# Seven-product matmul stage: product sums kept in PSUM, turns and cosines passed through PSUM, two tiles split at once

## The chip, the cores and the metric

One NeuronCore of a Trainium2 chip runs the whole kernel. The metric is the device time of one execution in microseconds. "PE" is TensorE, "ACT" ScalarE, "DVE" VectorE, "POOL" GpSimd, "SP" SyncE, which here only issues DMAs. Each engine works off its own queue of instructions in program order; between engines, semaphores hold an instruction until its inputs are there and its output buffer is free.

## The reference

```python
rms = np.sqrt(np.mean(x * x, axis=-1, keepdims=True) + 1e-06)      # for q and k: x / rms * g
scores = (1 / np.sqrt(64)) * np.matmul(q_n, k_n.transpose(0, 1, 3, 2))
attn = softmax(scores);  attn_out = np.matmul(attn, v)             # 8 batches, 12 heads, 448 x 64
x = attn_out.transpose(0, 2, 1, 3).reshape(8 * 448, 768)
h = x @ w_in                                                        # 768 -> 2048
g = h * np.cos(h)
return g @ w_out                                                    # 2048 -> 768
```

All tensors are float32.

## The kernel before, in words

**Two stages.** The first stage does the attention of all eight batches (48 units of two heads) and, batch by batch, the first layer `h = x @ w_in`, whose 16 blocks of 128 x 448 per batch go to a DRAM tensor `h_d`. The first layer of the last batch stands at the head of the second stage (`ffn1_block`, 16 blocks of 18 matmuls). The second stage reads `h_d`, forms `g = h cos h`, and multiplies it by `w_out`.

**Float32 through splits.** A float32 operand is split into a high part in a rounded format, which ACT writes (a copy), and the low rest, which POOL writes (a subtraction of two SBUF tiles). A product of two operands is three matmuls: high-high, high-low, low-high (`ffn2`, lines 627 to 629).

**Seven products in place of eight.** Batches are taken in pairs (`pr`, four of them). The left-hand matrix (`w_out`, transposed) and the right-hand one (`g` of two batches) are each cut into 2 x 2 parts, and Strassen's scheme in Winograd's form makes the four output parts from seven products `pi`, each summing over 8 blocks `k`, for three output blocks `oc` of 128 rows. So there are 4 x 7 x 8 x 3 x 3 = 2016 matmuls. The four parts of `g` are the roles a, b, d, c; each has 8 blocks, held as four tiles of two blocks (128 x 896) with names `B{home}_{g}`. Sums and differences of the parts (`g_mix`, line 607) are written in place over tiles that are no longer needed. The combined weights of the seven products are prepared during the first stage (`weights2`: loads of 384 KB on SP, decoding on DVE and ACT, mixes and splits on POOL and ACT, stores to `wo_d`), and loaded from there (`v_place`, line 279, 768 KB each, into 16 slots that the first layer's weights have left). Products 0 and 1 keep their weights; those of the other five are loaded for each pair.

**One tile of g.** `gl_load` (line 577) brings two blocks of h into one of three `hb` buffers. `g_turns` (582, ACT) writes round(h / 2 pi) as integers to SBUF. `g_reduce` (589 and 594, DVE) subtracts the turns times 2 pi in two steps. `g_cos` (598 and 599, ACT) takes the absolute value and the sine of pi/2 minus it. `g_mul` (603, DVE) multiplies by h and so frees `hb`. Every one of these works on 128 x 896.

**Splits and outputs.** `g_split` (616 ACT, 614 POOL) splits one block of 448 at a time, in rings of five high and four low tiles. Each product's three sums have PSUM banks of their own out of a ring of eight. `e_copy` (646, ACT) copies three of the products to SBUF, `e_add` (651, 653, DVE) adds four others from PSUM to SBUF tiles, and `e_sum` (657, DVE) adds SBUF tiles to SBUF tiles, nine times per pair. `e_store` (661) stores the outputs.

**Order.** The order of the instructions on every engine is fixed beforehand by a planner (`Plan`): each part has an engine, a cost, a due time, the data that it reads and writes, and rings of buffers; a greedy simulation with these costs takes, whenever an engine is free, the part that is ready with the earliest due time. In the second stage a block of `k` is given 1.83 us on PE (`PART`), a product 14.64 us (`PROD`); `D[pi]` is when product `pi` is due.

Of the kernel before, what the change touches and what calls it, by code (L numbers as in the profile page):

```python
# [126 lines left out]
def tile_attention_moe(  # L127
# [452 lines left out]
    def g_turns(pr, role, g):  # L580
        n = blk[(pr, role, g, "n")] = gpool.tile([128, NG, S], I32, tag="n", name=f"n{pr}{role}{g}", bufs=RING2["n"])
        nc.scalar.activation(n, gts[(pr, role, g)], AF.Copy, scale=1.0 / (2.0 * math.pi))

    def g_reduce(pr, role, g, step):
        if step == 0:
            t = blk[(pr, role, g)] = gpool.tile(
                [128, NG, S], F32, tag=f"B{home(pr, role)}_{g}", name=f"B{pr}{role}{g}", bufs=1
            )
            nc.vector.scalar_tensor_tensor(  # L589
                t, blk[(pr, role, g, "n")], -C1, gts[(pr, role, g)], op0=ALU.mult, op1=ALU.add  # L590
            )
        else:
            t = blk[(pr, role, g)]
            nc.vector.scalar_tensor_tensor(t, blk.pop((pr, role, g, "n")), -C2, t, op0=ALU.mult, op1=ALU.add)  # L594

    def g_cos(pr, role, g):
        t = blk[(pr, role, g)]
        nc.scalar.activation(t, t, AF.Abs)
        nc.scalar.activation(t, t, AF.Sin, bias=halfpi, scale=-1.0)

    def g_mul(pr, role, g):
        t = blk[(pr, role, g)]
        nc.vector.tensor_tensor(t, t, gts.pop((pr, role, g)), ALU.mult)  # L603

    def g_mix(pr, to, a, c, g, eng):
        t = blk[(pr, to, g)]
        eng.tensor_tensor(t, blk[(pr, a, g)], blk[(pr, c, g)], ALU.subtract)  # L607

    def g_split(pr, pi, role, k, lo):
        t = gpool.tile([128, S], F32R, tag="glo" if lo else "ghi", name=f"g{lo}{pr}{pi}{k}", bufs=RING2["glo" if lo else "ghi"])  # L610
        ops[(pr, pi, k, lo)] = t
        src = blk[(pr, role, k // NG)][:, k % NG, :]
        if lo:
            nc.gpsimd.tensor_tensor(t, src, ops[(pr, pi, k, 0)].bitcast(F32), ALU.subtract)  # L614
        else:
            nc.scalar.copy(t, src)  # L616

    def ffn2(pr, pi, k, slot):
        hi, lo = ops.pop((pr, pi, k, 0)), ops.pop((pr, pi, k, 1))
        w = wts[("wo", slot)][:, k % 2]  # L620
        for oc in range(NO):
            if k == 0:
                ys[(pr, pi, oc)] = ps_y.tile([128, 512], F32, tag="y", name=f"y{pr}_{pi}_{oc}")
            y = ys[(pr, pi, oc)][:, :S]
# [2 lines left out]
            nc.tensor.matmul(y, whi, hi, start=(k == 0), stop=False)  # L627
            nc.tensor.matmul(y, whi, lo, start=False, stop=False)  # L628
            nc.tensor.matmul(y, wlo, hi, start=False, stop=(k == NH - 1))  # L629
# [15 lines left out]
    def e_copy(pr, pi, oc, name):
        nc.scalar.copy(e_tile(pr, name, oc), ys.pop((pr, pi, oc))[:, :S])

    def e_add(pr, pi, oc, to, a, op):
        y = ys.pop((pr, pi, oc))[:, :S]
        if op == ALU.add:  # L650
            nc.vector.tensor_tensor(e_tile(pr, to, oc), y, e_tile(pr, a, oc), op)  # L651
        else:
            nc.vector.tensor_tensor(e_tile(pr, to, oc), e_tile(pr, a, oc), y, op)

    def e_sum(pr, oc, to, a, eng):
# [1 line left out]
        eng.tensor_tensor(t, t, e_tile(pr, a, oc), ALU.add)  # L657
# [236 lines left out]
    count = iter(range(1000))  # L894
    split_n = iter(range(1000))

    def block(pr, role, g, d):
# [6 lines left out]
        add(ACT, 0.95, d - 20.0, g_turns, pr, role, g, r=[hb], w=[t])
        add(DVE, 1.15, d - 17.0, g_reduce, pr, role, g, 0, r=[hb, t], w=[B_])
        add(DVE, 1.15, d - 16.0, g_reduce, pr, role, g, 1, r=[t], w=[B_])
        add(ACT, 2.0, d - 14.0, g_cos, pr, role, g, w=[B_])
        add(DVE, 1.2, d - 11.0, g_mul, pr, role, g, r=[hb], w=[B_])

    def mix(pr, to, a, c, g, eng, d):  # L910
        e, cost = (nc.vector, 1.2) if eng == DVE else (nc.gpsimd, 2.4)
        add(eng, cost, d, g_mix, pr, to, a, c, g, e,
            r=[("B", home(pr, x), g) for x in (a, c) if x != to], w=[("B", home(pr, to), g)])

    def product(pr, pi, role):
        d0 = T0 + PROD * (NPR * pr + pi)
        for kk in range(NH // 2):
            if pi >= 2 or pr == 0:
                s = slot(pr, pi, kk)
                add(SP, ISS, d0 + 2 * PART * kk - 24.0, v_place, pr, pi, kk, s, w=[("w", s)], land=8.0)  # L920
        for k in range(NH):
# [1 line left out]
            n = next(split_n)
            B_, hi, lo = ("B", home(pr, role), k // NG), ("ghi", n), ("glo", n)
            add(ACT, 0.53, d - 7.0, g_split, pr, pi, role, k, 0, r=[B_], w=[hi])
            add(POOL, 1.25, d - 5.0, g_split, pr, pi, role, k, 1, r=[B_, hi], w=[lo])
# [4 lines left out]
    def Y(pr, pi, oc):
        return NFC + NO * (NPR * pr + pi) + oc

    def copies(pr, pi, name, d):
        for oc in range(NO):
            add(ACT, 0.53, d + oc, e_copy, pr, pi, oc, name, r=[("y", Y(pr, pi, oc))], w=[(name, oc)])

    def sums(pr, pi, to, a, op, d, where=None):
        for oc in range(NO):
            add(DVE, 0.65, d + oc, e_add, pr, pi, oc, to, a, op,  # L940
                r=[("y", Y(pr, pi, oc))] + ([(a, oc)] if a != to else []), w=[(to, oc)])
            if where:
                add(SP, ISS, d + oc + 1, e_store, pr, oc, to, *where, r=[(to, oc)], land=LAND)

    def more(pr, to, a, d, eng, where=None):
        e, cost = (nc.vector, 0.65) if eng == DVE else (nc.gpsimd, 1.25)
        for oc in range(NO):
            add(eng, cost, d + oc, e_sum, pr, oc, to, a, e, r=[(a, oc)], w=[(to, oc)])
# [3 lines left out]
    for pr in range(NPAIR):  # L952
        D = [T0 + PROD * (NPR * pr + pi) for pi in range(NPR + 1)]
        gs_ = range(NGR)
        for role, pi in (("a", 0), ("b", 1), ("d", 2), ("c", 5)):
            for g in gs_:
                block(pr, role, g, D[pi] + BLOCK * g - (9.0 if role != "a" else 0.0))
        copies(pr, 0, "e1", product(pr, 0, "a") + 2)
        for g in gs_:
            mix(pr, "a", "b", "a", g, DVE, D[1] + BLOCK * g - 10.0)  # L960
        copies(pr, 1, "e5", product(pr, 1, "a") + 2)
        for g in gs_:
            mix(pr, "b", "d", "b", g, POOL, D[2] + BLOCK * g - 12.0)
        copies(pr, 2, "e7", product(pr, 2, "b") + 2)
        for g in gs_:
            mix(pr, "a", "d", "a", g, DVE, D[4] + BLOCK * g - 14.0)
        sums(pr, 3, "e3", "e5", ALU.add, product(pr, 3, "d") + 2)
        d = product(pr, 4, "a") + 2
        sums(pr, 4, "u", "e1", ALU.add, d)
        more(pr, "e3", "u", d + 3, DVE, (0, 1))  # L970
        more(pr, "e7", "u", d + 5, DVE)
        more(pr, "e5", "e7", d + 7, DVE, (1, 1))
        for g in gs_:
            mix(pr, "a", "a", "c", g, DVE, D[6] + BLOCK * g - 14.0)
        sums(pr, 5, "e1", "e1", ALU.add, product(pr, 5, "c") + 2, (0, 0))
# [51 lines left out]
```

## Time and profile before

| | us |
|---|---|
| median of 3 runs | 1553.64 (1552.02 to 1555.42) |
| the profiled execution | 1550.64 |
| its span, first to last instruction | 1548.9 |
| first matmul of the last batch's first layer / of the seven products | 980 / 1038.6 |
| last matmul | 1545 |

Mean granted TensorE clock: 0.98 of full speed. The profile gives, for each group of instructions of one line, the count, the duration and who released the engine when it had been idle. `y<-g,wo` are the matmuls of the seven products, `ph<-xs,wi` those of the first layer, `B2c` is the tile of pair 2, role c, `n2c` its turns, `g<-B2c` its split, `es` and `e` are output tiles.

### The profile page before, as it was taken

How to read it: one execution, taken by the hardware profiler on the slowest of the kernel's cores; microseconds unless marked ns; L12 is line 12 of the kernel's file. 1: busy time of each engine (PE TensorE's matmuls, PEld its weight loads, DVE VectorE, ACT ScalarE, POOL GpSimd, SP SyncE). 2: the span in 40 equal slices, each digit the busy share in tenths (PEclk: the TensorE clock that was granted, in tenths of full speed). 3: DMA queues.
4: the chain of work that ended last, by engine and by line, in shares of the span. 5: the costliest groups of instructions: out<-in, count | busy, mean ns of one | idle time of the engine just before them, and what ended most of it. 6: DMA issues, size and time to landing. Idle time of an engine off the chain costs nothing. (4 is left out here: it accounts for less than half of the span.)

```text
span 1548.9 us, 23023 instructions
## 1 busy us (share of the span) xinstructions
PE 1441.8 (93%) x7404; PEld 1180.7 (76%) x7404; DVE 1224.9 (79%) x1935; ACT 993.9 (64%) x2022; POOL 1109.0 (72%) x862
## 2 busy tenths in 40 slices
PE   7898998999999999999999999998988998798799
PEld 3446886787788788788788888897777887687698
DVE  7878999888778777878785554469899899899944
ACT  5767776777677766777766664565655655575442
POOL 5778878888868776767774531219869978887975
PEclk9999999999999999999999999999989999999999
DMA  6577334666456555455453321691774566368153
GB/s 209 172 213 231 100 105 151 208 201 204 155 182 194 163 178 169 149 185 187 154 170 127 97 74 52 223 356 55 265 245 143 182 217 247 100 231 304 64 190 132
DMA packets 137961, 270.43 MB, mean 175 GB/s; under 512 B 20768, under 2 KB 89200, under 8 KB 137840
## 3 DMA queue, kind: packets, MB, share of 16 engines
q1 hardware_dynamic: 137840, 268.96, 53.0%
q8 instruction: 58, 0.95, 0.3%
q14 instruction: 63, 0.52, 0.1%
HBM read 206.18 MB, written 62.73 MB: 174 GB/s over the span
## 5 line engine op out<-in xcount | busy, mean ns | idle before, releaser
L628 PE MATMUL y<-g,wo 128*128 128x448 f32 x672 | 262.9, 391 | 47.5 <-POOL g L614 47.5
L554 PE MATMUL ph<-xs,wi 128*128 128x448 f32 x768 | 298.5, 389 | 2.6 <-ACT he L566 2.6
L555 PE MATMUL ph<-xs,wi 128*128 128x448 f32 x768 | 282.0, 367 | 0.0
L556 PE MATMUL ph<-xs,wi 128*128 128x448 f32 x768 | 281.5, 367 | 0.0
L448 ACT ACTIVATE P<-S,sm 128x448 f32<-128x448 f32 x336 | 213.9, 641 | 92.1 <-DVE S L435 82.8
L627 PE MATMUL y<-g,wo 128*128 128x448 f32 x672 | 254.5, 379 | 11.4 <-ACT g L616 11.4
L629 PE MATMUL y<-g,wo 128*128 128x448 f32 x672 | 254.3, 378 | 0.0
L435 DVE TENSOR_SCALAR_CACHE_REDUCE S<-S,nr 128x448 f32<-128x448 f32 x336 | 218.6, 684 | 17.7 <-PE S L428 16.4
L484 ACT CAST hi<-PT 128x448 fp32r<-128x448 f32 x336 | 164.7, 536 | 88.4 <-PE PT L473 48.8
L492 DVE TENSOR_TENSOR lo<-PT,hi 128x448 fp32r<-128x448 f32 x252 | 145.4, 616 | 78.9 <-ACT hi L484 75.5
L628 PEld LDWEIGHTS y<-g,wo 128*128 128x128 f32 x672 | 132.3, 197 | 79.7 <-POOL g L614 69.2
L473 PEld LDWEIGHTS PT<-ident,P 128*128 128x128 f32 x1344 | 157.9, 142 | 32.0 <-issue 20.3
L473 PE MATMUL PT<-ident,P 128*128 128x128 f32 x1344 | 182.0, 276 | 0.0
L554 PEld LDWEIGHTS ph<-xs,wi 128*128 128x128 f32 x768 | 144.9, 189 | 31.7 <-issue 12.3
L556 PEld LDWEIGHTS ph<-xs,wi 128*128 128x128 f32 x768 | 144.5, 188 | 12.6
L555 PEld LDWEIGHTS ph<-xs,wi 128*128 128x128 f32 x768 | 145.3, 189 | 9.6
L627 PEld LDWEIGHTS y<-g,wo 128*128 128x128 f32 x672 | 132.1, 197 | 25.4 <-ACT g L616 13.6
L306 POOL TENSOR_TENSOR r<-r,nhalf 128x14 f32<-128x14 f32 (+1 forms) x50 | 128.6, 2576 | 31.1 <-DVE r L302 17.1
L629 PEld LDWEIGHTS y<-g,wo 128*128 128x128 f32 x672 | 132.4, 197 | 10.4
L509 PE MATMUL O<-hi,vs 128*128 128x448 f32 x336 | 111.9, 383 | 8.4 <-DVE hi L494 5.2
L509 PE MATMUL O<-lo,vs 128*128 128x448 f32 x252 | 99.6, 404 | 17.0 <-DVE lo L492 16.5
L371 POOL TENSOR_TENSOR kl<-kd,khi 128x448 fp32r<-128x448 f32 x46 | 55.7, 1210 | 67.1 <-ACT khi L367 67.0
(224 smaller groups left out, 3157.9 us busy)
## 6 DMA issues: line engine op xcount, KB each, us to landing
wo<-wo_d SPq DMA_DIRECT2D x88, 768.0 KB
h_d<-he SPq DMA_DIRECT2D x128, 224.0 KB
hb<-h_d SPq DMA_DIRECT2D x64, 448.0 KB
wo_d<-wv SPq DMA_DIRECT2D x56, 384.0 KB
sd<-sd SPq DMA_DIRECT2D x46, 448.0 KB
vd<-v SPq DMA_DIRECT2D x84, 160.0 KB
qd<-qT SPq DMA_DIRECT2D x48, 256.0 KB
raw<-w_in SPq DMA_DIRECT2D x16, 768.0 KB
```

Source lines behind the costliest of these rows:

```text
L435: nc.vector.tensor_scalar(d["S", t][:, :S], d["S", t][:, :S], d["nr"][:, t : t + 1], None, op0=ALU.mult, op1=ALU.min, accum_out=d["sm"][:, ...
L448: nc.scalar.activation(tl(u, f"P{t}", [128, S], F32, "P"), d.pop(("S", t))[:, :S], AF.Exp, bias=sm[:, 1, t : t + 1], scale=-1.0, accum_out ...
L473: nc.tensor.transpose(pt[:, t * 128 : t * 128 + 128], src, ident)
L484: nc.scalar.copy(hi, pt[:, hh * S : hh * S + S])
L492: nc.vector.tensor_tensor(lo, src, hi.bitcast(F32), ALU.subtract)
L509: nc.tensor.matmul(O, st, d.pop((what, kb, hh)), start=(kc + n == 0), stop=(kc + n == 4))
L554: nc.tensor.matmul(ph[:, :S], whi, x2[:, 0, :], start=(cc == 0), stop=False)
L555: nc.tensor.matmul(ph[:, :S], whi, x2[:, 1, :], start=False, stop=False)
L556: nc.tensor.matmul(ph[:, :S], wlo, x2[:, 0, :], start=False, stop=(cc == NCC - 1))
L627: nc.tensor.matmul(y, whi, hi, start=(k == 0), stop=False)
L628: nc.tensor.matmul(y, whi, lo, start=False, stop=False)
L629: nc.tensor.matmul(y, wlo, hi, start=False, stop=(k == NH - 1))
```

## The change

The seven products are taken in another order (1, 7, 6, 2, 5, 4, 3 in place of 1, 5, 7, 3, 6, 2, 4). Product 0 starts a sum in one set of three PSUM banks; products 2, 4 and 6 go on adding to that same sum (`CHAIN` is 2: no start flag), and it is read in between. Products 1, 3 and 5 start afresh in the other set. The two sets change places with each pair. There are 6 named banks for sums (the first layer uses them too) in place of a ring of 8.

The two banks left over hold the turns and the cosines of one block of 448 at a time: ACT writes them to PSUM, and DVE reads them from there. Only the absolute value is still taken on 896. The SBUF tiles for turns go.

Splits take two blocks (128 x 896) at once, in rings of three. The additions of SBUF tiles to SBUF tiles for the outputs go; in the last pair the last output tile is copied in two halves by ACT and DVE. One of the four mixes is now an addition; the one on POOL is the last one (a - c), where it was d - b. The blocks b and d are due together, 18 us ahead of product 1, c 12 us ahead of product 3. The weights of the second stage are prepared from unit 18 to unit 46 of the plan in place of 12 to 45.

```diff
-    ORDER = (1, 5, 7, 3, 6, 2, 4)
+    ORDER = (1, 7, 6, 2, 5, 4, 3)
...
-            ffn1(b, fc, part, ps_y, "y")
+            ffn1(b, fc, part, ps_y, f"y{fc % NB}")
...
-    def g_turns(pr, role, g):
-        n = blk[(pr, role, g, "n")] = gpool.tile([128, NG, S], I32, tag="n", name=f"n{pr}{role}{g}", bufs=RING2["n"])
-        nc.scalar.activation(n, gts[(pr, role, g)], AF.Copy, scale=1.0 / (2.0 * math.pi))
+    def g_turns(pr, role, g, f):
+        n = gts[(pr, role, g, f)] = ps_g.tile([128, 512], I32, tag="n", name=f"n{pr}{role}{g}{f}")
+        nc.scalar.activation(n[:, :S], gts[(pr, role, g)][:, f, :], AF.Copy, scale=1.0 / (2.0 * math.pi))
...
+        t = blk[(pr, role, g)][:, f, :]
+        n = gts[(pr, role, g, f)][:, :S]
+        src = t if step else gts[(pr, role, g)][:, f, :]
+        nc.vector.scalar_tensor_tensor(t, n, -C2 if step else -C1, src, op0=ALU.mult, op1=ALU.add)
+
+    def g_abs(pr, role, g):
         t = blk[(pr, role, g)]
         nc.scalar.activation(t, t, AF.Abs)
-        nc.scalar.activation(t, t, AF.Sin, bias=halfpi, scale=-1.0)
+
+    def g_cos(pr, role, g, f):
+        c = gts[(pr, role, g, f)] = ps_g.tile([128, 512], F32, tag="c", name=f"c{pr}{role}{g}{f}")
+        nc.scalar.activation(c[:, :S], blk[(pr, role, g)][:, f, :], AF.Sin, bias=halfpi, scale=-1.0)
+
+    def g_mul(pr, role, g, f):
+        c, h = gts.pop((pr, role, g, f)), gts[(pr, role, g)][:, f, :]
+        nc.vector.tensor_tensor(blk[(pr, role, g)][:, f, :], c[:, :S], h, ALU.mult)
...
+    def g_split(pr, pi, role, g, lo):
+        name = "glo" if lo else "ghi"
+        t = ops[(pr, pi, g, lo)] = gpool.tile([128, NG, S], F32R, tag=name, name=f"{name}{pr}{pi}{g}", bufs=RING2[name])
+        src = blk[(pr, role, g)]
         if lo:
-            nc.gpsimd.tensor_tensor(t, src, ops[(pr, pi, k, 0)].bitcast(F32), ALU.subtract)
+            nc.gpsimd.tensor_tensor(t, src, ops[(pr, pi, g, 0)].bitcast(F32), ALU.subtract)
...
-            nc.tensor.matmul(y, whi, hi, start=(k == 0), stop=False)
-            nc.tensor.matmul(y, whi, lo, start=False, stop=False)
-            nc.tensor.matmul(y, wlo, hi, start=False, stop=(k == NH - 1))
+            nc.tensor.matmul(y, whi, hi, start=(k == 0 and chain < 2), stop=False, skip_group_check=chain == 2)
+            nc.tensor.matmul(y, whi, lo, start=False, stop=False, skip_group_check=chain == 2)
+            nc.tensor.matmul(y, wlo, hi, start=False, stop=(k == NH - 1), skip_group_check=chain == 2)
...
-    def e_sum(pr, oc, to, a, eng):
-        t = e_tile(pr, to, oc)
-        eng.tensor_tensor(t, t, e_tile(pr, a, oc), ALU.add)
...
-        span = (base(NU - NP // 2) - base(2 * NP)) / NH
-        d0 = base(2 * NP) + k * span
+        span = (base(NU - 2) - base(3 * NP)) / NH
+        d0 = base(3 * NP) + k * span
...
-    RING2 = {"he": 2, "hb": 3, "n": 2, "ghi": 5, "glo": 4, "y": 8}
+    RING2 = {"he": 2, "hb": 3, "ghi": 3, "glo": 3, "n": 1, "c": 1}
+    CHAIN = (0, 1, 2, 1, 2, 1, 2)
...
+        return 3 if role == "b" else ("acd".index(role) + pr) % 3
+
+    def bank(pr, pi, oc):
+        return NO * ((pr + CHAIN[pi] % 2) % 2) + oc
...
+        for f in range(NG):
+            t = ("n", NG * n + f)
+            add(ACT, 0.56, d - 20.0 + 1.5 * f, g_turns, pr, role, g, f, r=[hb], w=[t])
+            add(DVE, 0.63, d - 19.0 + 1.5 * f, g_reduce, pr, role, g, f, 0, r=[hb, t], w=[B_])
+            add(DVE, 0.63, d - 18.5 + 1.5 * f, g_reduce, pr, role, g, f, 1, r=[t], w=[B_])
+        add(ACT, 0.96, d - 15.0, g_abs, pr, role, g, w=[B_])
+        for f in range(NG):
+            c = ("c", NG * n + f)
+            add(ACT, 0.57, d - 13.0 + 1.5 * f, g_cos, pr, role, g, f, r=[B_], w=[c])
+            add(DVE, 0.63, d - 12.0 + 1.5 * f, g_mul, pr, role, g, f, r=[hb, c], w=[(*B_, f)])
...
+        for roles, pi, ahead in (("a", 0, 12.0), ("bd", 1, 18.0), ("c", 3, 12.0)):
+            for g in range(NGR):
+                for n, role in enumerate(roles):
+                    block(pr, role, g, D[pi] + BLOCK * g - ahead + 2 * n)
+        d = product(pr, 0, "a")
+        mix(pr, "b", "d", "b", ALU.subtract, D[1] - 12.0)
+        copies(pr, 0, "e1", d + 1)
+        mix(pr, "a", "b", "a", ALU.add, D[2] - 14.0)
+        d = product(pr, 1, "b")
+        copies(pr, 1, "e7", d + 1)
+        d = product(pr, 2, "a")
+        mix(pr, "b", "d", "a", ALU.subtract, D[3] - 10.0)
+        sums(pr, 2, "u3", "e7", d + 1)
+        mix(pr, "a", "c", "a", ALU.subtract, D[3] - 2.0, POOL)
+        d = product(pr, 3, "c")
+        sums(pr, 3, "e1", "e1", d + 1, (0, 0))
+        d = product(pr, 4, "b")
+        sums(pr, 4, "c22", "e7", d + 1, (1, 1))
+        d = product(pr, 5, "a")
+        sums(pr, 5, "u3", "u3", d + 1, (1, 0))
+        d = product(pr, 6, "d")
+        copies(pr, 6, "c12", d + 1, (0, 1))
```

More of the change, by code (lines that the diff above doesn't have):

```diff
@@ L587, in g_reduce @@
+    def g_reduce(pr, role, g, f, step):
+        if (step, f) == (0, 0):
+            blk[(pr, role, g)] = gpool.tile(
                 [128, NG, S], F32, tag=f"B{home(pr, role)}_{g}", name=f"B{pr}{role}{g}", bufs=1
             )
[L589 to L594, printed above, removed]
@@ L618, in ffn2 @@
     def ffn2(pr, pi, k, slot):
-        hi, lo = ops.pop((pr, pi, k, 0)), ops.pop((pr, pi, k, 1))
+        hi, lo = (ops[(pr, pi, k // NG, x)][:, k % NG, :] for x in range(2))
         w = wts[("wo", slot)][:, k % 2]
+        chain = CHAIN[pi]
         for oc in range(NO):
-            if k == 0:
-                ys[(pr, pi, oc)] = ps_y.tile([128, 512], F32, tag="y", name=f"y{pr}_{pi}_{oc}")
-            y = ys[(pr, pi, oc)][:, :S]
+            bk = bank(pr, pi, oc)
+            if k == 0 and chain < 2:
+                ys[bk] = ps_y.tile([128, 512], F32, tag=f"y{bk}", name=f"y{pr}_{pi}_{oc}")
+            y = ys[bk][:, :S]
             whi = w[:, 0, oc * 128 : oc * 128 + 128]
             wlo = w[:, 1, oc * 128 : oc * 128 + 128]
-            nc.tensor.matmul(y, whi, hi, start=(k == 0), stop=False)
-            nc.tensor.matmul(y, whi, lo, start=False, stop=False)
-            nc.tensor.matmul(y, wlo, hi, start=False, stop=(k == NH - 1))
+            nc.tensor.matmul(y, whi, hi, start=(k == 0 and chain < 2), stop=False, skip_group_check=chain == 2)
+            nc.tensor.matmul(y, whi, lo, start=False, stop=False, skip_group_check=chain == 2)
+            nc.tensor.matmul(y, wlo, hi, start=False, stop=(k == NH - 1), skip_group_check=chain == 2)
     es = {}
@@ L641, in e_tile, with e_copy, e_add @@
                     es["t"] = xpool.tile([128, 2 * NCC, S], F32, tag="xs", name="es")
-                es[(pr, name, oc)] = es["t"][:, NO * ("e7", "e3", "u").index(name) + oc, :]
+                es[(pr, name, oc)] = es["t"][:, NO * ("u3", "c12", "c22").index(name) + oc, :]
         return es[(pr, name, oc)]
[L645 to L651, printed above, removed]
-        else:
-            nc.vector.tensor_tensor(e_tile(pr, to, oc), e_tile(pr, a, oc), y, op)
-    def e_sum(pr, oc, to, a, eng):
-        t = e_tile(pr, to, oc)
-        eng.tensor_tensor(t, t, e_tile(pr, a, oc), ALU.add)
+    def e_copy(pr, pi, oc, name, hf=None):
+        t, y = e_tile(pr, name, oc), ys[bank(pr, pi, oc)][:, :S]
+        if hf is not None:
+            t, y = (x[:, hf * S // 2 : hf * S // 2 + S // 2] for x in (t, y))
+        if hf == 1:
+            nc.vector.tensor_copy(t, y)
+        else:
+            nc.scalar.copy(t, y)
+    def e_add(pr, pi, oc, to, a):
+        nc.vector.tensor_tensor(e_tile(pr, to, oc), ys[bank(pr, pi, oc)][:, :S], e_tile(pr, a, oc), ALU.add)
     def e_store(pr, oc, name, i, j):
@@ L886, in tile_attention_moe @@
         d = BLOCK * fc
-        add(PE, BLOCK, d, ffn1_block, B - 1, fc, w=[("y", fc), ("w", fc)])
-        add(ACT, 0.53, d + 4.0, h_out, B - 1, fc, r=[("y", fc)], w=[("he", fc)])
+        y = ("y", fc % NB)
+        add(PE, BLOCK, d, ffn1_block, B - 1, fc, w=[y, ("w", fc)])
+        add(ACT, 0.53, d + 4.0, h_out, B - 1, fc, r=[y], w=[("he", fc)])
         add(SP, ISS, d + 5.0, h_store, B - 1, fc, r=[("he", fc)], w=[("hd", B - 1, fc)], land=LAND)
@@ L892, in slot @@
         return 4 * pi + kk if pi < 2 else 8 + (20 * pr + 4 * (pi - 2) + kk) % 8
-    count = iter(range(1000))
-    split_n = iter(range(1000))
+    count, split_n = iter(range(1000)), iter(range(1000))
     def block(pr, role, g, d):
@@ L899, in block, with block_keys, mix @@
         n = next(count)
-        hb, t = ("hb", n), ("n", n)
-        B_ = ("B", home(pr, role), g)
+        hb, B_ = ("hb", n), ("B", home(pr, role), g)
         r = [("hd", 2 * pr + j, NH * i + NG * g + f) for f in range(NG)]
         add(SP, ISS, d - 30.0, gl_load, pr, role, g, r=r, w=[hb], land=LAND)
[L904 to L913, printed above, removed]
+        for f in range(NG):
[8 more added lines that the diff above has]
+            add(DVE, 0.63, d - 12.0 + 1.5 * f, g_mul, pr, role, g, f, r=[hb, c], w=[(*B_, f)])
+    def block_keys(pr, role, g):
+        B_ = ("B", home(pr, role), g)
+        return [B_] + [(*B_, f) for f in range(NG)]
+    def mix(pr, to, a, c, op, d, eng=DVE):
+        e, cost = (nc.vector, 1.2) if eng == DVE else (nc.gpsimd, 2.3)
+        for g in range(NGR):
+            add(eng, cost, d + BLOCK * g, g_mix, pr, to, a, c, g, op, e,
+                r=sum((block_keys(pr, x, g) for x in (a, c) if x != to), []), w=block_keys(pr, to, g))
     def product(pr, pi, role):
@@ L919, in product @@
                 s = slot(pr, pi, kk)
-                add(SP, ISS, d0 + 2 * PART * kk - 24.0, v_place, pr, pi, kk, s, w=[("w", s)], land=8.0)
+                add(SP, ISS, d0 + BLOCK * kk - 24.0, v_place, pr, pi, kk, s, w=[("w", s)], land=8.0)
         for k in range(NH):
             d = d0 + PART * k
[L923 to L926, printed above, removed]
+            g = k // NG
@@ L927, in product @@
+            if k % NG == 0:
+                n = next(split_n)
+                Bs, hi, lo = block_keys(pr, role, g), ("ghi", n), ("glo", n)
+                add(ACT, 0.96, d - 8.0, g_split, pr, pi, role, g, 0, r=Bs, w=[hi])
+                add(POOL, 2.3, d - 6.0, g_split, pr, pi, role, g, 1, r=Bs + [hi], w=[lo])
             s = slot(pr, pi, k // 2)
-            add(PE, PART, d, ffn2, pr, pi, k, s, r=[hi, lo, ("w", s)], w=[("y", Y(pr, pi, oc)) for oc in range(NO)])
+            add(PE, PART, d, ffn2, pr, pi, k, s, r=[hi, lo, ("w", s)], w=[("y", bank(pr, pi, oc)) for oc in range(NO)])
@@ L929, in product, with copies @@
         return d0 + PROD
-    def Y(pr, pi, oc):
-        return NFC + NO * (NPR * pr + pi) + oc
-    def copies(pr, pi, name, d):
+    def copies(pr, pi, name, d, where=None):
         for oc in range(NO):
-            add(ACT, 0.53, d + oc, e_copy, pr, pi, oc, name, r=[("y", Y(pr, pi, oc))], w=[(name, oc)])
-    def sums(pr, pi, to, a, op, d, where=None):
-        for oc in range(NO):
[L940 to L948, printed above, removed]
+            y = ("y", bank(pr, pi, oc))
+            if where and pr == NPAIR - 1 and oc == NO - 1:
+                add(ACT, 0.3, d + oc, e_copy, pr, pi, oc, name, 0, r=[y], w=[(name, oc)])
+                add(DVE, 0.35, d + oc, e_copy, pr, pi, oc, name, 1, r=[y], w=[(name, oc, 1)])
+            else:
+                add(ACT, 0.53, d + oc, e_copy, pr, pi, oc, name, r=[y], w=[(name, oc)])
@@ L949, in more, with sums @@
+            if where:
+                add(SP, ISS, d + oc + 1, e_store, pr, oc, name, *where, r=[(name, oc), (name, oc, 1)], land=LAND)
+    def sums(pr, pi, to, a, d, where=None):
+        for oc in range(NO):
+            add(DVE, 0.63, d + oc, e_add, pr, pi, oc, to, a,
+                r=[("y", bank(pr, pi, oc))] + ([(a, oc)] if a != to else []), w=[(to, oc)])
             if where:
@@ L953, in tile_attention_moe @@
         D = [T0 + PROD * (NPR * pr + pi) for pi in range(NPR + 1)]
[L954 to L975, printed above, removed]
-        sums(pr, 6, "e7", "e7", ALU.subtract, product(pr, 6, "a") + 2, (1, 0))
+        for roles, pi, ahead in (("a", 0, 12.0), ("bd", 1, 18.0), ("c", 3, 12.0)):
+            for g in range(NGR):
+                for n, role in enumerate(roles):
[18 more added lines that the diff above has]
+        copies(pr, 6, "c12", d + 1, (0, 1))
     with tc.manual_schedule():
```

26 lines of the change are left out of this document (8 added, 18 removed).

## The prediction

> **What bounds the kernel now.** First the page's share of the span by engine and its 40 slices; then busy time by stage, the waits of the second stage, single lines, and the timeline at one wait.
>
> ```profile
> PE 1441.8 (93%) x7404; PEld 1180.7 (76%) x7404; DVE 1224.9 (79%) x1935; ACT 993.9 (64%) x2022; POOL 1109.0 (72%) x862
> PE   7898998999999999999999999998988998798799
> DVE  7878999888778777878785554469899899899944
> ```
>
> PE is at 93%, but a matmul's busy time overlaps the next one's, so I count matmuls per stretch (the x after PE). Columns: stretch, its length, busy time of PE, PEld, DVE, ACT, POOL, granted clock, DMA share, GB/s.
>
> ```profile
> 240.00:260.00 20.00, 15.39 (x82) 12.02 (x83) 19.23 (x36) 13.44 (x31) 19.25 (x17) 1.00 0.49 150
> 260.00:280.00 20.00, 17.10 (x91) 13.88 (x90) 17.46 (x34) 12.62 (x29) 16.46 (x15) 1.00 0.49 159
> 355.00:829.00 474.00, 463.49 (x2610) 382.89 (x2610) 364.65 (x799) 336.58 (x782) 352.43 (x326) 0.99 0.55 173
> 440.00:460.00 20.00, 20.00 (x116) 16.72 (x115) 15.46 (x38) 14.19 (x32) 11.16 (x11) 1.00 0.57 185
> 980.00:1038.60 58.60, 58.60 (x285) 53.21 (x284) 33.45 (x30) 38.22 (x52) 7.84 (x5) 1.00 0.93 324
> 1038.60:1545.20 506.60, 447.71 (x2018) 390.73 (x2016) 436.47 (x295) 277.70 (x420) 413.75 (x236) 0.95 0.54 185
> 1520.00:1540.00 20.00, 20.00 (x101) 18.53 (x100) 8.57 (x9) 5.41 (x10) 13.18 (x11) 1.00 0.27 97
> ```
>
> The change's home is 1038.6 to 1545.2: 2016 matmuls of the 28 products. Undisturbed matmuls follow each other so:
>
> ```profile
> 1538.13 0.36 PE L629 MATMUL y<-g,wo 128*128 128x448 f32 x1
> ...
> 1544.21 0.36 PE L629 MATMUL y<-g,wo 128*128 128x448 f32 x1
> ```
>
> Thirty matmuls in 6.08 us: 0.2027 apart. 2016 × 0.2027 = 408.6; the stage takes 506.6, so 98.0 us are lost in it. Who holds PE there (waiter, what it waited for, us, times, longest):
>
> ```profile
> PEld y L628 <- POOL g L614: 69.2, 74, 4.1
> POOL g L614 <- ACT g L616: 53.1, 26, 7.4
> PEld y L627 <- ACT g L616: 13.6, 6, 3.7
> ```
>
> 82.8 us of waiting, and behind a wait the clock is slow as well (the stage's mean grant is 0.95):
>
> ```profile
> 1206.97 0.37 PE L627 MATMUL y<-g,wo 128*128 128x448 f32 x1
> 1210.10 0.47 PE L628 MATMUL y<-g,wo 128*128 128x448 f32 x1 [2.76 <-POOL g L614]
> ...
> 1210.97 0.57 PE L628 MATMUL y<-g,wo 128*128 128x448 f32 x1
> ...
> 1213.58 0.57 PE L629 MATMUL y<-g,wo 128*128 128x448 f32 x1
> ```
>
> Seven matmuls in 2.61 us are 0.373 apart. So the splits come late, because POOL and ACT are late, because of DVE. Columns: min/median/max in ns.
>
> ```profile
> L589 DVE SCALAR_TENSOR_TENSOR B0b<-n0b,hb x4: 1086/1092/1092, 1011.4 to 1027.7; 128x896 f32<-128x896 int32 x4
> L589 DVE SCALAR_TENSOR_TENSOR B0c<-n0c,hb x4: 1720/2032/3011, 1066.5 to 1089.5; 128x896 f32<-128x896 int32 x4
> L607 DVE TENSOR_TENSOR B1a<-B1b,B1a x4: 2035/2042/2555, 1168.5 to 1187.2; 128x896 f32<-128x896 f32 x4
> L607 POOL TENSOR_TENSOR B1b<-B1d,B1b x4: 2142/2956/2961, 1171.5 to 1205.2; 128x896 f32<-128x896 f32 x4
> L614 POOL TENSOR_TENSOR g<-B1a,g x32: 1149/1996/2024, 1164.1 to 1290.3; 128x448 fp32r<-128x448 f32 x32
> L657 DVE TENSOR_TENSOR es<-es x24: 611/1570/1580, 1137.3 to 1521.6; 128x448 f32<-128x448 f32 x24
> L651 DVE TENSOR_TENSOR es<-y,e x24: 605/610/625, 1117.8 to 1516.0; 128x448 f32<-128x448 f32 x24
> L492 DVE TENSOR_TENSOR lo<-PT,hi x252: 601/615/626, 124.5 to 963.8; 128x448 fp32r<-128x448 f32 x126
> ```
>
> The same DVE operation takes 1.09 us while POOL is nearly idle (before 1038) and 2.03 beside POOL's splits; POOL's take 1.15 or 2.00. Each slows the other when DVE reads two SBUF tiles. With one operand in PSUM (L651, L492) DVE never passes 0.626, whatever POOL does. The bound of the stage is this mutual slowing: DVE is busy 86% of it, POOL 82%.
>
> **The change, part by part**, per pair of batches (7 products, 504 matmuls, 102.2 us of PE; now 506.6/4 = 126.65).
>
> *Turns and cosines through PSUM.* 16 blocks had 48 DVE operations on 896 elements; now 96 on 448 with the turn or cosine read from PSUM. No row has scalar_tensor_tensor on integers from PSUM. Nearest are L651's 0.610 and, against it, L657's 1.570 (two SBUF tiles): I take 0.613, as one operand is in PSUM. 96 × 0.613 = 58.8 us. Undisturbed, two halves cost 1.22 against 1.09, so alone this adds 0.13 × 48 = 6.2 us; it pays only through the disturbance. [...]
>
> *Mixes.* Twelve on DVE (2.04 each beside POOL: 24.5) and four on POOL, as before; another one is POOL's.
>
> *Sums in PSUM.* L657 goes, nine a pair; the 12 additions from PSUM stay: 7.4. The banks of one product are written again two products later. Three copies or additions have the product between (14.6 us) as cover; without it PE would wait for three of 0.6.
>
> DVE per pair: 58.8 + 24.5 + 7.4 = 90.7, against (33.5 + 436.5)/4 = 117.5.
>
> *Splits of two tiles.* POOL: 28 of 896. Not shown; L607's 2.14 at the least disturbed and twice 1.149 are near: 2.3. With four mixes 74, plus 10 for those running beside 24.5 us of DVE mixes (24.5 × (1 − 1.15/2.0)): 84, against 105.4. ACT:
>
> ```profile
> L314 ACT ACTIVATE PT<-sd x4: 547/548/548, 3.4 to 12.1; 128x448 f32<-128x448 f32 x4
> L598 ACT ACTIVATE B0a<-B0a x4: 952/954/956, 987.4 to 1007.5; 128x896 f32<-128x896 f32 x4
> L599 ACT ACTIVATE B0a<-B0a,halfpi x4: 1045/1047/1047, 989.7 to 1008.5; 128x896 f32<-128x896 f32 x4
> L646 ACT COPY e<-y x24: 521/530/547, 1059.2 to 1476.9; 128x448 f32<-128x448 f32 x24
> ```
>
> 28 × 0.954 + 32 × 0.548 (turns, written to PSUM) + 16 × 0.954 + 32 × 0.60 (half a sine, in L599's ratio) + 9 × 0.53 = 83. PE's 102.2 becomes the longest.
>
> *New waits.* One bank for turns, one for cosines: a turn waits until both reductions of the half before it have read the bank; behind it in ACT's queue stand the splits that PE needs. Hand-over shows as 0.09 us (ACT to DVE):
>
> ```profile
> 1417.98 0.95 ACT L582 ACTIVATE n3d<-hb 128x896 int32<-128x896 f32 x1 [1.02 <-DMA hb<-h_d]
> ...
> 1419.02 1.09 DVE L589 SCALAR_TENSOR_TENSOR B3d<-n3d,hb 128x896 f32<-128x896 int32 x1 [1.19 <-ACT n3d L582]
> ```
>
> A half holds its bank 0.55 + 1.23 + 0.18 = 1.96 us; 32 make 63 of 102, hidden unless DVE has something longer ahead. The splits' rings (three of two tiles) give 11 us of cover; if that is gone, PE waits and then runs at 0.373.
>
> Blocks b and d are now due together, 18 us ahead of product 1, and c 12 ahead of product 3: eight loads of hb stand in SP's queue in a row, among the weight loads. Pair 0 has the 58.6 us of first-layer matmuls as cover (DVE 33.5 busy there), the others the three products since their homes came free; if that is gone, product 1 waits for its first mix. The mix left to POOL (a − c, 2.3 each) queues ahead of splits; the same 11 us cover it.
>
> *Weights of the second stage* are prepared later and more tightly (span 66.5 for 78.4 in the plan, six attention units later): 32 loads and 56 stores on SP, 88 POOL, 128 DVE and 88 ACT operations move with it. At the old start PE made 82 and 91 matmuls for 116 in 20 us: 5.9 + 4.3 = 10.2 us lost. Ends: all of it regained (−10), or lost twice (+10); I take −3, since later stretches have DVE freer. Their last store moves by some 19 us from 829, far ahead of the second stage.
>
> *Order of products, bank names:* nothing; the loads of weights only change slots. *Tail:* the last tile is copied in halves, 0.3 us less.
>
> *Sum.* Residual loss: in 355 to 829, with DVE 77% busy, PE made 2610 of the 2749 that 116 per 20 us allow: 5.1% lost. With DVE at 89% of PE's time I take between as much and half as much again, 6.3%: 408.6/0.937 = 436. Span: 1548.9 − (506.6 − 436) − 3 − 0.3 = 1475.0; with the 1.7 us around it (1550.64 − 1548.9) 1476.7. The profiled execution is 3.0 under the median of the runs, 1553.64; I put the forecast between the two scales, **1478**. Its own range is 1450 (no loss: 1548.9 − 98 − 3 + 1.7) to 1500.
>
> **Rivals.** *A: the hb ring binds.* Three buffers; a load's passage:
>
> ```profile
> 1410.48 7.47 DMA hb<-h_d
> 1418.02 10.37 DMA hb<-h_d
> ```
>
> ```profile
> SPq L577 <- DVE B2c L603: 27.9, 4, 16.1
> ```
>
> 7 to 10 us until it is used, then 7.7 us of its own work (two turns 1.1, four reductions 2.45, 0.95, 2 × 1.2, nine hand-overs 0.8), and what stands ahead in the queues. It decides once a passage is over 19.2 us (3 × 102.2/16). With 10.4 + 7.7 + two mixes of 2.04 it is 22.2, 118 us a pair, 473 for the stage: 1514. For it: loads queue behind 768 KB weight loads. SP already waits up to 16.1 us for a product to free a buffer. Against: those passages were stretched by a slow DVE.
>
> *B: no relief, slower.* The reductions on integers keep taking the shared path. 64 × 1.57 + 32 × 0.613 + 24.5 + 7.4 = 152 us of DVE a pair; scaled by 126.65/117.5 the pace is 164, +149 in all: about 1700. It turns from faster to slower once the 96 halves average over 0.89 us ((117.5 − 31.9)/96). Against: 252 + 24 rows from PSUM, none over 0.626. [...]
>
> *C: the change does not do what it says*: splits stay the bound, POOL at 896 elements being disturbed as a whole, 4 us each: 28 × 4 + 10 = 122 us a pair, about today's 126.65: 1550. Against: DVE reads two SBUF tiles in only 24.5 of 102 us.
>
> **How the numbers follow.** Forecast 0.67, A 0.2, B 0.06, C 0.07. Holding eight in ten means the forecast's range and most of A: 1450 to 1516. The runs of before spread over 3.4 us, 0.2%, which is what can be told from no change. Faster: 0.67 + 0.2 + 0.03 of C = 0.90; same 0.03; slower 0.07.
>
> **What would show it.** Right: reductions and products near 0.61 each, splits on POOL near 2.3, at least 95 matmuls per 20 us in most stretches, DVE below 90%, clock above 0.97 in the second stage, no L657. Wrong: halves at 1 us or more (B); POOL's splits at 3 or more (C); loads of hb waiting long for the products that free them, and turns waiting for them (A); or ACT's turns standing for DVE with PE's waits shifted from POOL to ACT.

## The result, and the profile after

The changed kernel takes 1458.64 us (median of 4 runs, 1457.63 to 1460.19) where the kernel before takes 1553.37 beside it: a ratio of 0.939, with a 95% interval of 0.9374 to 0.9406. The forecast was 1478, in a range of 1450 to 1516; the profiled execution is 1460.19, its span 1458.2. First the page: busy time by engine, and the slices of PE, DVE and POOL.

```profile
PE 1408.1 (97%) x7404; PEld 1167.4 (80%) x7404; DVE 1069.7 (73%) x2092; ACT 1001.4 (69%) x2038; POOL 973.9 (67%) x750
PE   6898999999999999999999999999999999999998
DVE  7878999678788687878687756536876876976821
POOL 5779779777787867796787573101296596685674
```

The holes at the end of PE's line are gone, although PE does the same work. The same stretches as before, with the same columns (stretch, length, busy time of PE, PEld, DVE, ACT, POOL with their counts, granted clock, DMA share, GB/s):

```profile
1030.80:1454.20 423.40, 415.66 (x2018) 379.43 (x2016) 288.93 (x425) 283.00 (x421) 278.29 (x125) 1.00 0.66 222
1132.00:1236.00 104.00, 102.38 (x506) 94.54 (x505) 80.17 (x121) 77.81 (x118) 71.43 (x32) 1.00 0.73 247
1160.00:1180.00 20.00, 18.38 (x91) 16.71 (x90) 17.30 (x24) 15.82 (x25) 16.68 (x7) 1.00 0.39 120
240.00:260.00 20.00, 17.92 (x95) 13.76 (x95) 15.51 (x36) 16.09 (x37) 19.83 (x18) 1.00 0.45 134
260.00:280.00 20.00, 19.66 (x112) 16.09 (x112) 14.00 (x31) 12.64 (x30) 14.43 (x13) 1.00 0.51 157
355.00:829.00 474.00, 465.20 (x2619) 384.14 (x2618) 371.15 (x815) 342.63 (x794) 359.66 (x332) 1.00 0.57 181
```

The first row is the product stage: 423.4 us for the 2016 matmuls that took 506.6, so 83.2 of the 90.7 us that the span lost are here. The stage starts 7.8 us earlier (1030.8 for 1038.6); the 82 and 91 matmuls of the two stretches from 240 to 280 have become 95 and 112. DVE's busy time in the stage fell from 436 to 289 us, POOL's from 414 to 278, and the granted clock rose from 0.95 to 1.00. The second row is about one pair of batches (506 matmuls). Next, single lines by count, min/median/max in ns:

```profile
L592 DVE SCALAR_TENSOR_TENSOR B1a<-n1a,hb x8: 610/620/625, 1080.1 to 1098.7; 128x448 f32<-128x448 int32 x8
L592 DVE SCALAR_TENSOR_TENSOR B1a<-n1a,B1a x8: 624/624/626, 1080.8 to 1099.3; 128x448 f32<-128x448 int32 x8
L604 DVE TENSOR_TENSOR B1a<-c1a,hb x8: 611/618/625, 1087.3 to 1105.8; 128x448 f32<-128x448 f32 x8
L607 DVE TENSOR_TENSOR B1a<-B1b,B1a x4: 1081/1089/1478, 1136.1 to 1163.3; 128x896 f32<-128x896 f32 x4
L607 DVE TENSOR_TENSOR B1b<-B1d,B1a x4: 1079/1914/2979, 1155.2 to 1168.9; 128x896 f32<-128x896 f32 x4
L614 POOL TENSOR_TENSOR glo<-B1a,ghi x12: 2120/2130/2993, 1132.8 to 1220.4; 128x896 fp32r<-128x896 f32 x12
```

Every operation that reads a turn or a cosine from PSUM takes 0.61 to 0.63, whatever POOL does. The mixes, which still read two SBUF tiles, stand at 1.09 when POOL is between splits and reach 2.98 beside one; a split reaches 2.99. Most of them now miss each other. What PE still waits for in the stage (waiter, released by, us in total, times, longest):

```profile
PEld y L630 <- POOL glo L614: 8.7, 4, 2.9
PEld y L629 <- ACT ghi L616: 0.9, 1, 0.9
```

Before, POOL's splits held it for 69.2 us. One of the four waits in the timeline (start, duration, engine, operation):

```profile
1163.29 3.01 POOL L614 TENSOR_TENSOR glo<-B1b,ghi 128x896 fp32r<-128x896 f32 x1 [6.46 <-ACT ghi L616]
...
1163.27 1.08 DVE L607 TENSOR_TENSOR B1a<-B1b,B1a 128x896 f32<-128x896 f32 x1
1164.27 2.98 DVE L607 TENSOR_TENSOR B1b<-B1d,B1a 128x896 f32<-128x896 f32 x1
...
1166.35 0.47 PE L630 MATMUL y<-glo,wo 128*128 128x448 f32 x1 [1.62 <-POOL glo L614]
```

The first mix began 0.02 us before the split and took its 1.08 us undisturbed; the split took 0.88 over its 2.13. The second mix began during the split and ended 0.95 us after it (1167.25 against 1166.30), about a whole mix later. In these rows they take turns, and the matmul that needs the split is 1.62 us late. In the third window row above (1160 to 1180) that shows as 91 matmuls where the stretch after it has 100.

### The profile page after: what moved, and what is told of

It reads as the page before. It is cut to its first block, busy times and chain, and to the rows that moved or that the text cites. A ratio compares the mean times of both kernels' runs of the same rounds, so it can differ in the third digit from the quotient of the medians.

```text
span 1458.2 us, 22829 instructions
## 1 busy us (share of the span) xinstructions
PE 1408.1 (97%) x7404; PEld 1167.4 (80%) x7404; DVE 1069.7 (73%) x2092; ACT 1001.4 (69%) x2038; POOL 973.9 (67%) x750
## 4 chain that ended last, share of the span: by engine, by line
PE 70%; DVE 11%; ACT 4%; issue 3%; POOL 3%; DMA 1%; SPq 0%; ACTq 0%; DVEq 0%; POOLq 0%
PE ph L554 9%; PE ph L555 8%; PE ph L556 8%; PE O L509 8%; PE y L630 8%; PE y L631 8%; PE y L629 7%; PE PT L473 7%; PE S L428 6%; DVE S L435 2%; ACT hi L484 1%; DVE lo L492 1%; DVE hi L494 1%; DVE xf L526 1%; POOL glo L614 1%
## 5 line engine op out<-in xcount | busy, mean ns | idle before, releaser
L448 ACT ACTIVATE P<-S,sm 128x448 f32<-128x448 f32 x336 | 213.8, 640 | 92.9 <-DVE S L435 83.2
L630 PE MATMUL y<-glo,wo 128*128 128x448 f32 x672 | 247.4, 368 | 7.3 <-POOL glo L614 7.3
L629 PE MATMUL y<-ghi,wo 128*128 128x448 f32 x672 | 247.1, 368 | 0.5 <-ACT ghi L616 0.5
L631 PE MATMUL y<-ghi,wo 128*128 128x448 f32 x672 | 247.0, 368 | 0.0
L630 PEld LDWEIGHTS y<-glo,wo 128*128 128x128 f32 x672 | 126.6, 188 | 20.2 <-POOL glo L614 8.7
L629 PEld LDWEIGHTS y<-ghi,wo 128*128 128x128 f32 x672 | 126.6, 188 | 12.3 <-ACT ghi L616 0.9
L631 PEld LDWEIGHTS y<-ghi,wo 128*128 128x128 f32 x672 | 126.6, 188 | 11.4
L428 PE MATMUL S<-khi,qhi 64*128 64x448 f32 (+1 forms) x350 | 99.9, 491 | 1.5 <-ACT khi L343 1.2
```

What stands on the lines that cost most here:

```text
L428: nc.tensor.matmul(d["S", t][:, :S], d[a][p0:p1, j * 128 : j * 128 + 128], d[c][p0:p1, :], start=(n == 0), stop=(n == len(ops) - 1),)
L448: nc.scalar.activation(tl(u, f"P{t}", [128, S], F32, "P"), d.pop(("S", t))[:, :S], AF.Exp, bias=sm[:, 1, t : t + 1], scale=-1.0, accum_out ...
L629: nc.tensor.matmul(y, whi, hi, start=(k == 0 and chain < 2), stop=False, skip_group_check=chain == 2)
L630: nc.tensor.matmul(y, whi, lo, start=False, stop=False, skip_group_check=chain == 2)
```

## The experiments

Unless said otherwise, ratios are to the kernel before on the same chip, with their 95% interval.

**Is it the route through PSUM?** Both turns and cosines back in SBUF, all else as changed:

```diff
-        n = ... ps_g.tile([128, 512], I32, tag="n", ...)
+        n = ... gpool.tile([128, S], I32, tag="n", ..., bufs=1)
-        c = ... ps_g.tile([128, 512], F32, tag="c", ...)
+        c = ... gpool.tile([128, S], F32, tag="c", ..., bufs=1)
```

> The changed kernel with one thing undone: turns and cosines go through SBUF tiles of 448 (one buffer each) in place of PSUM banks; counts, order and rings stay. Theory (the gain is that DVE, with one operand in PSUM, no longer waits for POOL's splits nor holds them up): the 96 half operations a pair go from 0.62 us to 1.0 or more on average, POOL's splits from 2.13 to 2.6 or more, DVE to 95% of the product stage, and the time to 1530 or more. Rival (halves, the order of products and the fewer additions give the gain, PSUM is only a place): under 1475.

1581.0 us, 1.0177 (1.0155 to 1.02): 122 us over the changed kernel, and slower than before. Of this kernel: the stage's window, two lines, and PE's waits.

```profile
1031.40:1576.20 544.80, 453.15 (x2017) 394.99 (x2015) 450.22 (x429) 285.50 (x424) 292.20 (x125) 0.94 0.51 174
...
L592 DVE SCALAR_TENSOR_TENSOR B1a<-n1a,hb x8: 612/1367/2546, 1094.1 to 1123.1; 128x448 f32<-128x448 int32 x8
L592 DVE SCALAR_TENSOR_TENSOR B1d<-n1d,B1d x8: 624/1504/2495, 1136.3 to 1195.5; 128x448 f32<-128x448 int32 x8
...
PEld y L630 <- POOL glo L614: 93.3, 55, 4.1
```

The minimum is the same 0.61 as from PSUM; only beside POOL do the halves go to 2.5: of the 91 over 0.7 us that the timeline shows singly from 1090 to 1500, 89 overlap an operation of POOL. In the changed kernel (1080 to 1400) none of 290 is over 0.7, though 237 overlap one. DVE's count hardly differs (429 for 425 operations), yet it is busy 450 us for 289. So the mutual slowing is the cause, and the PSUM operand takes it away. Two sizes of the expectation were missed: DVE is busy 83% of the stage, not 95%, and a split on POOL averages 2.35 us (256.5 for 109), not 2.6. It is mainly DVE that waits, and PE waits for splits although POOL is busy only 54% of the stage. With the turns alone in SBUF:

> As the kernel with both in SBUF, but the cosines stay in PSUM: only the two reductions (64 of 96 halves a pair) read two SBUF tiles. Theory of the shared path: the reductions 1.0 us or more, the products still 0.61; the loss lies at half to four fifths of that with both in SBUF, 1495 to 1560. Rival (place does not matter): under 1475. If the loss is already as large as with both, the reductions alone fill DVE.

1552.79 us, 0.9996 (0.9983 to 1.0008), within the expected range. In this kernel's lines the two kinds of operation stand beside the same POOL:

```profile
L592 DVE SCALAR_TENSOR_TENSOR B1a<-n1a,hb x8: 618/1334/2094, 1095.2 to 1119.2; 128x448 f32<-128x448 int32 x8
L604 DVE TENSOR_TENSOR B1a<-c1a,hb x8: 617/618/625, 1105.0 to 1126.7; 128x448 f32<-128x448 f32 x8
```

The cosines from PSUM stay at 0.62 while the turns from SBUF do not. Undone in this order, the 64 operations a pair that read turns carry 94 us, and the 32 that read cosines another 28; what the cosines alone would cost was not run.

**The route alone, on the kernel before** (order, sums, single splits and weights as before; a ring of six banks for `y`):

```diff
-    def g_turns(pr, role, g):            # 896 to SBUF; g_reduce, g_cos, g_mul likewise
+    def g_turns(pr, role, g, f):         # 448 to PSUM, as in the change
-    RING2 = {..., "n": 2, "ghi": 5, "glo": 4, "y": 8}
+    RING2 = {..., "n": 1, "c": 1, "ghi": 5, "glo": 4, "y": 6}
```

> The kernel before with the PSUM route alone: turns and cosines of 448 through two banks, six banks in place of eight for sums; old order, additions in SBUF, splits of one tile, old timing of the weights. Theory (the route is the main part): DVE a pair 58.8 + 12 mixes at up to 2.0 + 7.4 + 9 additions near 1.0 = 99 of PE's 102, so most of the 95 us come, 1480 to 1505. Rival (the parts are worth something only together, six banks for sums cost a wait): 1530 or more.

1476.73 us, 0.9508 (0.9482 to 0.9534). Its stage:

```profile
1039.90:1467.40 427.50, 416.92 (x2017) 379.57 (x2015) 322.30 (x460) 295.43 (x531) 313.48 (x236) 0.99 0.65 219
```

Some 77 of the 95 us come from the route alone, a little more than expected (1480 us at best).

**The weights.** The schedule of before put back into the changed kernel, and the new one put into the kernel before:

```diff
-        span = (base(NU - 2) - base(3 * NP)) / NH
-        d0 = base(3 * NP) + k * span
+        span = (base(NU - NP // 2) - base(2 * NP)) / NH
+        d0 = base(2 * NP) + k * span
```

> The changed kernel with the old timing of the second stage's weights (from unit 12). Theory (the product stage began 7.8 us sooner because the first stage lost less where these weights used to begin): 1464 to 1469, and the matmuls from 240 to 280 fall back from 207 to about 173. Rival (the 7.8 us come from elsewhere): 1457 to 1461.

> The kernel before with the new timing of the second stage's weights alone. Theory: 1543 to 1548, product stage still some 506 us long. Rival: no change, 1551 to 1556.

1468.39 us (0.9451, 0.9435 to 0.9466) and 1544.15 us (0.9944, 0.9932 to 0.9957): the later preparation is worth 9.7 us in the one kernel and 0.56% of 1554, 8.7 us, in the other. In the first of them the matmuls from 240 to 280 fall to 167 (expected 173, with the late weights 207).

**Do the parts add up?** Route and late weights on the kernel before:

> The kernel before with two parts of the change: turns and cosines through two PSUM banks (six for y), and the weights of the second stage after two blocks rather than one. If the parts simply add up, 1476.7 less the 8.7 to 9.9 us of the weights: 1465 to 1469 us. Rival: the product stage, moved 8 us earlier, runs into loads that it did not meet before (or drops ones that it did), and the sum does not hold: below 1463 or over 1471.

1467.42 us, 0.9451 (0.9431 to 0.947): they do. What is left to the changed kernel, 9 us, belongs to the order (with its due times and mixes), the chain of banks and the splits.

**Splits of one tile** in the changed kernel, in rings of six (as many tiles in all):

```diff
-        t = ... gpool.tile([128, NG, S], F32R, tag=name, ...)
+        t = ... gpool.tile([128, S], F32R, tag=name, ...)
-    RING2 = {..., "ghi": 3, "glo": 3, ...}
+    RING2 = {..., "ghi": 6, "glo": 6, ...}
-            if k % NG == 0: ...
+            add(ACT, 0.53, d - 8.0, g_split, pr, pi, role, k, 0, r=Bs, w=[hi])
+            add(POOL, 1.15, d - 6.0, g_split, pr, pi, role, k, 1, r=Bs + [hi], w=[lo])
```

> The changed kernel with splits of one tile again (rings of six in place of three double ones). Theory: POOL 56 x 1.16 = 65 us a pair in place of 28 x 2.13 = 60, of 102, ACT 5 us more: hidden, 1456 to 1466. Rival (the splits' length was a bound): 1475 or more. Second rival (shorter splits hold DVE's mixes up for less, and come sooner): 1450 to 1455.

1452.21 us, 0.9357 (0.9337 to 0.9377). Stage and waits:

```profile
1030.50:1445.90 415.40, 414.01 (x2017) 378.10 (x2015) 283.87 (x425) 298.21 (x529) 297.34 (x234) 1.00 0.67 226
...
PEld y L630 <- POOL glo L614: 3.3, 6, 1.4
```

The expectation "hidden" fell: POOL has 19 us more to do, and the kernel is some 6 us faster, since a late split holds PE for 1.4 us at most, not 2.9. DVE's mixes in the stage come out shorter too (1.45 us on average for 1.52), as the second rival has it, and its range was met. The two intervals overlap by a hair (0.9377 and 0.9374); the pairs below support the sign.

**The chain undone.** The sums of product 2, 4 and 6 start afresh, and VectorE adds them in SBUF (six more SBUF+SBUF additions a pair, and three from PSUM in place of copies), in the new order:

```diff
-            nc.tensor.matmul(y, whi, hi, start=(k == 0 and chain < 2), ...)
+            nc.tensor.matmul(y, whi, hi, start=(k == 0), stop=False)
...
+            add(DVE, 0.63, d + oc, e_sum, pr, oc, to, a, c, op, ...)
```

> The changed kernel without the chain of banks: every product starts its banks afresh, and DVE makes the sums (six additions of two SBUF tiles and three from PSUM more a pair; three copies fewer on ACT). Theory: 6 to 11 us of DVE a pair in about 24 us of slack: hidden, 1458 to 1468. Rival (keeping the sums in PSUM is a main part of the gain): 1480 or more.

1482.86 us, 0.9554 (0.9539 to 0.957): 24 us more, not hidden. Of this kernel one 20 us stretch, and the group of the new additions (count, busy us, mean ns, idle before):

```profile
1271.80:1291.80 20.00, 11.86 (x42) 10.08 (x43) 18.75 (x23) 11.81 (x18) 11.58 (x5) 0.74 0.21 59
...
L660 DVE TENSOR_TENSOR es<-es,e 128x448 f32<-128x448 f32 x24 | 34.0, 1471 | 0.0
```

The loss stands once in each pair after the first, around product 1, where the last blocks b and d and three mixes fall: DVE 18.75 of 20 us busy, POOL 11.58, 42 matmuls for 98. The additions read two SBUF tiles, so they are stretched to 1.47 us on average (0.61 at the least, 2.56 at the most) and delay the blocks: the first reduction of pair 2's b runs 186.2 us into the stage (1218.0 less 1031.8), in the changed kernel 175.3 (1206.3 less 1031.0). Part of these 10.9 us is the loss of the pair before; but PE has made 860 matmuls by then for 829, so against the matmuls that need it the block starts about 6 us later (31 at 0.2027). The kernel with the route alone has nine such additions a pair and a stage of only 427.5, so the additions alone can't be it. To tell VectorE's load from the long splits, the same with splits of one tile:

> The chain of banks undone (block sums in SBUF, six more SBUF+SBUF additions a pair) and one tile to a split. With splits of two tiles the sums in SBUF cost 24 us, nearly all of it once a pair around product 1. Theory A: POOL's two-tile splits and the additions that read two SBUF operands hold each other up there; with splits half as long the loss mostly goes: under 1462 us. Theory B: VectorE simply has more to do there than the time of two blocks, whatever the splits do: 1470 us or more. Between them: both have a part.

1465.96 us, 0.9437 (0.9417 to 0.9457): between the theories. Its stretch around product 1 of pair 2:

```profile
1260.00:1280.00 20.00, 15.10 (x62) 13.08 (x61) 19.68 (x26) 15.61 (x28) 11.01 (x8) 0.83 0.22 70
```

With single splits the sums in SBUF cost 12 to 14 us (by the ratios, and by 1466.0 less 1452.2), and there VectorE is full (19.68 of 20) while POOL has room: theory B's part. The other 10 or so of the 24 come only with the long splits: theory A's. Read the other way, splits of two tiles cost 17 us with the sums in SBUF (1482.9 less 1466.0) and 6 without.

**The ring of hb** with four buffers in place of three (`"hb": 4`):

> The changed kernel with four hb buffers in place of three. What is left of waiting in the product stage (about 10 us: 5 in the first pair, 1.6 in each later one) comes where the last blocks of b and d are late. If the passage of hb sets their pace (7.2 us a block, three buffers): 1450 to 1455. If DVE's mixes beside POOL do: 1457 to 1461.

1455.66 us, 0.9372 (0.9356 to 0.9388), against 0.939 (0.9374 to 0.9406): 3 us, not clear of nothing, and between the two answers expected. Together with single splits:

> The changed kernel with one tile to a split and a ring of four instead of three for the halves of b that come from HBM. Theory: a reduction waits for its transfer at the same places whatever the splits do, so the 1 to 3 us that the deeper ring took away come on top of the 6 us of the single splits: 1447 to 1452 us. Rival: with single splits TensorE no longer waits in the stage, so a shorter wait of a reduction ends nothing sooner: the time stays at 1451 to 1454 us.

1451.31 us, 0.9334 (0.9308 to 0.936), from runs of 1444.05 to 1453.5. Beside it, on the same chip, the changed kernel again:

> The changed kernel itself, beside its variants on the same chip: 1456 to 1461 us by every theory, ratio to before 0.937 to 0.941.

1458.21 us, 0.9388 (0.9365 to 0.9411). The two intervals are apart: this version beats both kernels, by 7 us the changed one. Whether the fourth buffer adds to single splits (1452.21) stays open; expectation and rival overlap at 1451.3. Its profiled run shows what is left in the stage:

```profile
1030.30:1440.90 410.60, 409.81 (x2015) 377.78 (x2013) 288.19 (x426) 294.15 (x532) 299.77 (x234) 1.00 0.68 229
```

The row begins two matmuls late; from the first, at 1029.9, the stage takes 411.0 us, against the 408.6 of 2016 undisturbed matmuls. In this execution hardly anything is left to gain there but by fewer matmuls.

The profiled stages in a row:

| kernel | start of the stage | its length |
|---|---|---|
| before | 1038.6 | 506.6 |
| route alone | 1039.9 | 427.5 |
| route and late weights | 1032.2 | 429.4 |
| and new order, sums in SBUF, single splits | 1031.9 | 428.0 |
| and the chain of banks | 1030.5 | 415.4 |
| and splits of two tiles (the change) | 1030.8 | 423.4 |

Each row is one execution. That of the changed kernel's second run has a stage of 419.4 us (1029.6 to 1449.0), so a step of 4 us between two rows means little. The order by itself shows no effect, the chain takes 12.6 us away, and the double splits give some 4 to 8 back.

## Why the prediction was right, and where its sizes were off

**What bounds the stage: right.** With the turns and cosines in SBUF the stage takes 544.8 us, through PSUM 423.4, with the same instructions otherwise. Rival B (the reductions stay slowed) is refuted by 0.604 to 0.627 for every reduction; rival C (splits stay the bound, 4 us each) by a median split of 2.13 us and POOL busy 66% of the stage.

Beside POOL's splits VectorE's operations took 0.61 to 0.63 us with one SBUF input, and up to 2.55 with two at the same size (the lines quoted above). Halving had its price: two halves are 1.24 for 1.09, so 48 of them cost 7 us a pair. It was paid, and was small beside what it bought.

The profiled time came out 16.5 us under the sum's 1476.7. That it was no more is partly luck: the sum gave the chain of banks nothing of its own and the double splits no cost, and these two errors offset each other in part. Term by term:

**Residual loss: the step that was mis-sized.** The sum took 6.3% (27.4 us), carried over from the attention stage; measured are 14.8 us, 3.5% (423.4 less 408.6). That is 12.6 of the 16.5 us. The attention stage still loses 4.7% (2619 matmuls of 2749 between 355 and 829), so its share did not carry over to this stage. Of the 14.8, PE's recorded waits make 7.8 (7.3 for POOL's splits and 0.5 for ACT's, in the matmul groups of the page), and the longer pitch of matmuls (last section) from 1280 on, some 840 matmuls by 0.0040 us, 3.4. The rest is not assigned; some of it is the slower clock behind the longest wait (87 matmuls at 0.91 from 1060 to 1080). In the second run of the same kernel only 10.8 us are lost (419.4 less 408.6), so the size of this term varies by some 4 us from one execution to the next.

**DVE: 80.2 us a pair for a forecast of 90.7.** Reductions and products came as costed (0.61 to 0.63 for 0.613). The mixes did not: twelve took 17.6 us in the pair from 1132 to 1236, 1.47 each for the 2.04 of before. The prediction took their slowing as it stood; but POOL, busy 66% of the stage where it was 82%, is no longer always beside them.

**POOL: 71.4 a pair for 84.** A split averages 2.26 (63.2 us for 28 in that window), as forecast at 2.3. The extra 10 us for running beside DVE's mixes was counted on top of a figure that already held it. ACT: 77.8 for 83.

**Sums in PSUM: costed only as fewer instructions of DVE, which is too little.** The six additions that the chain saves against the version in SBUF cost 12 to 14 us with single splits and 24 with double ones, since they fall where VectorE is full.

**Splits of two tiles: the wrong sign.** They were costed by POOL's total, with 11 us of rings as cover. The total did fall (278.3 us of POOL in the stage for 297.3), but the unit in which one engine holds up the other, and a delay reaches PE, doubled (a split of `B1a` takes 2.31 us on average for 1.20): 8.7 us of waits (7.1 in the second run) for 3.3, and about 6 us of time.

**Weights: −3 taken, −7.8 measured** at the stage's start, −8.7 and −9.7 by the experiments: near the end of −10 that the sum had kept. The 34 matmuls regained from 240 to 280 are 5.9 us of it at 116 in 20 us, and DVE, 19.23 of 20 us busy at the old start, now is 15.51. That row, with DVE and POOL (19.25) both full, was a reason to take more of that end.

**New waits, rival A.** The order of loads does bunch, and TensorE's remaining waits do stand once a pair at the last blocks of b and d. Loads did wait up to 10.4 us for a product with h to free their buffer (16.1 before), one of the signs named for A, yet turns waited for a load only 6.4 us in all. A fourth buffer gave some 3 us, not clear of nothing, where the rival priced the ring at 37 over the sum. Its passage of 10.4 + 7.7 + two mixes was put together from waits of a slow DVE, as the prediction itself held against it. The tail came at nothing instead of −0.3.

## What to carry to other kernels

When two engines slow each other, price the pair, not the instruction: look for the rows in which the same shape has two durations (here 1.09 and 2.03 us on VectorE, 1.15 and 2.00 on GpSimd), find what stands beside the long one, and try one operand in PSUM in place of SBUF, even if that means twice as many instructions: with 96 halves a pair for 48 whole ones, the route alone took the stage from 506.6 to 427.5 us. Merging the splits lowered GpSimd's total, from 297.3 to 278.3 us, and doubled the longest wait of TensorE for a late one, from 1.4 to 2.9; GpSimd had room, and the smaller unit was the better one. And additions that looked hidden were not: with them VectorE is busy 75% of the stage (331.4 of 444.8 us), but 18.75 of the 20 us in which they hold TensorE up.
